# Half of x turned by transposing DMA, a shorter unfold and a new order of the queues, in a fused FFT filter and state-space kernel

## The chip, the cores and the metric

The kernel runs on one core of a Trainium2 chip. The metric is the device time of one execution in microseconds (us), the median of several runs. In the profile, PE is TensorE, PEld its weight loads, DVE is VectorE, ACT is ScalarE, POOL is GpSimd and SP is SyncE, whose queue issues nearly all DMAs here.

## The reference, cut to what matters

```python
# x: (1, 2048, 1024), bf16; S = 2048 rows, D = 1024 columns
g = sigmoid((x * gate_w).sum(-1))               # one gate for each row
a = irfft2(rfft2(x) * (w_r + 1j * w_i))         # a filter over both axes
Lam_bar = exp(dt * Lam)                         # P = 1024 complex states
Bu = einsum("bld,pd->blp", x, B_bar)
h[t] = Lam_bar * h[t - 1] + Bu[t]               # along the 2048 rows
b = 2 * einsum("blp,dp->bld", h, C).real + x * Dskip
return g * a + (1 - g) * b
```

## The kernel before

All of it is one program in which two branches share the engines. Rows of x come in sixteen row tiles of 128 rows (`r`), four to a chunk of 512 rows (`c`). States come in eight blocks of 128 (`jb`).

**Start.** SP loads the row tiles into `xn` (L445) and the first block of B into `bn`. `turn` (L478) transposes a tile: eight 128x128 transposes on PE into PSUM (`pt`, L483), and one copy of the result into `xT[c]`, by DVE (L488) or ACT (L486) in turn. `halves(c)` (L499) folds the columns of `xT[c]` into `xpm` on DVE, with one small product on PE (`xps`, L516) and its cast on ACT (L518).

**State-space branch.** `bu` (L862) multiplies `xT[c]` by a block of B, `BTs`, into PSUM (`psu`, L872; sixteen 512-column matmuls for a block and a chunk). ACT casts the result into `h` (L875). DVE rotates it by a table `cs` (`rot`, L840 to L846), scans along the rows (L884) and rotates it back by a table `pn` (`rot_out`). `load_BT` (L856) loads the later blocks of B by transposing DMA (L859), and `load_CT` those of C (L826). `table` (L614) makes `cs` and `pn[:, jb]` for each block.

**Filter branch.** Stage one: `fd` transforms along the columns (`ps_fd`, L651 and L656, from all of `xpm`), ACT casts (L662), `s1` does the first half of the row transform (L671), ACT casts (L674), and SP writes the result to the DRAM scratch `turn1` (L675). Stage two: `s2w` reads it back turned (L756, into slots that lie in `h`), does the second half (`ps_s`, L762), ACT casts to X2 (L765), and DVE multiplies by W (L767); `fixup` mends the first column through `Bcol` (L714). `is1` and `is2` are the inverse transforms (L780, L799), with another trip through DRAM between them, and `idft` (L814) ends the branch: ACT scales by the gate (L819) and SP writes `ga_scratch`.

**Output.** `unfold` (L907) reads two row tiles of `ga_scratch` and rebuilds the full 1024 columns from even and odd parts with two operations of 1024 elements (L915) and four of 512 (L919), two of which write backwards. `yout` (L926) multiplies `h` by C (`ps_y`, L935), adds the Dskip term (`diag`, L943, or L953 and L954) and combines both branches (L962 with an accumulating DMA from POOL, or L971 on DVE).

**What sets the order.** Nothing runs as written. Every operation is put into a `Plan` with an engine, a key and an estimated time; `Plan.run` (L237) simulates the engines by these estimates, takes the operation with the smallest key among those that could start, and emits each engine's queue in that order. The keys are linear in the constants `K_...` (L387 to L433). Buffers come from groups of slots handed out in that simulated order: two large buffers `b32` (`xn`, `xpm`, then the two halves of `h`), four PSUM slots, and so on. `ORDER` hands them out in the order in which they were made:

```python
ORDER = ("b32", "b8", "tf", "tt", "bt", "cs")
```

On the chip each engine then runs its queue in order and waits on semaphores.

Of the kernel before, what the change touches and what calls it, by code (L numbers as in the profile page):

```python
# [14 lines left out]
BF16 = mybir.dt.bfloat16  # L15
# [283 lines left out]
def kernel(  # L299
# [17 lines left out]
    nc = tc.nc  # L317
    x = A_x[0]
# [11 lines left out]
    cpool = ctx.enter_context(tc.tile_pool(name="cpool", bufs=1))  # L330
# [39 lines left out]
    def pe(key, us, fn, r=(), w=()):  # L370
        plan.op("PE", key, us + 0.16, fn, r, w, gap=us)
# [4 lines left out]
    def dve(key, us, fn, r=(), w=()):  # L376
        plan.op("DVE", key, us, fn, r, w, gap=us - 0.085)
# [4 lines left out]
    def dma(key, us, fn, r=(), w=(), eng="SP", issue=0.38):  # L382
        plan.op(eng, key, 0.0, fn, r, w, gap=issue, dma=us)

    U = 0.216
    A2 = nc.scalar.activation
    K_T0 = 103.63  # L387
    K_TB = 92.88
    K_D = 2317.44
    K_O = -4292.69  # L390
    K_TAB0 = -89.94
    K_TAB = -755.34
    K_F0 = 261.54
    K_F = 15.56
    K_W0 = -3804.78
    K_W = 211.26
    K_WI = -1048.11
    K_I0 = -7430.02
    K_I = 31.36
    K_ID = 61.05  # L400
    K_CT = 287.45
    K_FIX = -6993.11
    K_R1 = 218.2
    K_R2 = 3273.35
    K_RS = -1.13
    K_Y = -2754.69
    K_YS = 362.25
    K_H = 358.12
    K_HM = 136.71
    K_XR = -109.14  # L410
    K_HP = 257.29
    K_XP = -155.54
    K_XS = -637.95
    K_TP = -327.41
    K_DM = 2752.64
    K_BT = -203.64
    K_UN = 4095.78
    K_WD = -299.06
    K_KA = -1.48
    K_KR = -90.54  # L420
    K_YL = 2318.0
    K_PC = 2539.19
    K_TL = 361.21
    K_TM = 642.41
    K_D1 = 138.38
    K_WC = 442.52
    K_FW = -3775.02
    K_SM = -4700.75
    K_R3 = 2855.54
    K_R4 = -1680.01  # L430
    K_D3 = 231.26
    K_SK = -768.95
    K_GATE = 1276.71  # L433
    KX = lambda c: K_XP * (c > 0) + K_XS * max(c - 1, 0)


    vec8 = tile_of([8, 5, P], BF16, "vec8", "tt")
    for i, src in enumerate((B_Lambda_re, B_Lambda_im, B_log_dt, gate_w, B_Dskip)):
        dma(0, 0.05, lambda i=i, src=src: nc.scalar.dma_start(out=vec8.t[:, i, :], in_=src.rearrange("(j p) -> j p", p=P)),
            w=[(vec8, i)], eng="ACT", issue=0.33)  # L440

    xn = tile_of([P, 16, D], BF16, "xn", "b32")
    bn = tile_of([P, 2, D], BF16, "bn", "b8")
    for r in range(16):
        dma(r, 0.8, lambda r=r: nc.sync.dma_start(out=xn.t[:, r, :], in_=x[P * r:P * (r + 1), :]), w=[(xn, r)])  # L445
# [17 lines left out]
    ident = cpool.tile([P, P], BF16, name="ident")  # L463
# [11 lines left out]
    xT = [xpool.tile([P, 8, TC], BF16, name=f"xT{c}") for c in range(NCH)]  # L475
    BTb = {0: tile_of([P, 2, 8, P], BF16, "BTs", "bt")}

    def turn(key, src, item, dst, ditem, on_act):  # L478
        pt = psum([P, 8, P], "pt", BF16)

        def f():
            for j8 in range(8):
                nc.tensor.transpose(out=pt.t[:, j8, :], in_=src()[:, P * j8:P * (j8 + 1)], identity=ident)  # L483
        pe(key, 8 * 0.06, f, r=[item, ("ident",)], w=[(pt,)])
        if on_act:
            act(key, 1.01, lambda: nc.scalar.copy(out=dst(), in_=pt.t), r=[(pt,)], w=[ditem])  # L486
        else:
            dve(key, 0.69, lambda: nc.vector.tensor_copy(out=dst(), in_=pt.t), r=[(pt,)], w=[ditem])  # L488

    def turn_x(c):  # L490
        for q in range(4):
            r = 4 * c + q
            turn(KX(c) + q, lambda r=r: xn.t[:, r, :], (xn, r), lambda c=c, q=q: xT[c][:, :, P * q:P * (q + 1)],
                 ("xT", c, q), q % 2)

    xT_of = lambda c: [("xT", c, q) for q in range(4)]
    xpm = tile_of([P, 2, 4, S], BF16, "xpm", "b32")

    def halves(c):  # L499
        lo, hi = xT[c][:, 0:4, :], xT[c][:, 4:8, :]  # L500
        both = tile_of([P, 4, TC], BF16, "both", "su")
        at = slice(TC * c, TC * (c + 1))
        dve(KX(c) + K_H, 1.22, lambda: nc.vector.tensor_add(out=both.t, in0=lo, in1=hi), r=xT_of(c), w=[(both,)])
        for g, fn in enumerate((nc.vector.tensor_add, nc.vector.tensor_sub)):
            dve(KX(c) + K_H, 0.69, lambda g=g, fn=fn: fn(out=xpm.t[:, 0, 2 * g:2 * g + 2, at], in0=both.t[:, 0:2, :], in1=both.t[:, 2:4, :]),
                r=[(both,)], w=[(xpm, c, 0, g)])
# [101 lines left out]
            r=[("gB",)], w=[("omg_bf",)])  # L608
        dve(key + 30, 0.2, lambda: nc.vector.tensor_copy(out=omg, in_=omg_bf), r=[("omg_bf",)], w=[("omg",)])


    pn = cpool.tile([P, NJB, 2, TC], BF16, name="pn")

    def table(jb, key):  # L614
        tt = tile_of([P, 2, TC], FP32, "tt", "tt")
# [291 lines left out]
    def unfold(tb, key):  # L907
        eo = tile_of([P, 2, 2, K], BF16, "eoc", "eoc")
        dma(key - K_DM, 1.5, lambda: nc.sync.dma_start(out=eo.t.rearrange("p s h k -> p s (h k)"),
                                                       in_=ga_dram[P * tb:P * (tb + 2), :].rearrange("(s p) n -> p s n", s=2)),  # L910
            r=[("ga", bp) for bp in range(16)], w=[(eo,)], issue=0.55)
        pq = tile_of([P, 2, 2, K], BF16, "pq", "pq")
        ga = tile_of([P, 2, D], BF16, "ga", "bt")
        for i, fn in enumerate((nc.vector.tensor_add, nc.vector.tensor_sub)):
            dve(key, 0.69, lambda i=i, fn=fn: fn(out=pq.t[:, i], in0=eo.t[:, :, 0, :], in1=eo.t[:, :, 1, :]), r=[(eo,)], w=[(pq, i)])  # L915
        for i in range(2):
            for j, fn in enumerate((nc.vector.tensor_add, nc.vector.tensor_sub)):
                cols = slice(K * j, K * j + 256) if i == 0 else slice(K * j + 511, K * j + 255, -1)
                dve(key, 0.42, lambda i=i, cols=cols, fn=fn: fn(out=ga.t[:, :, cols], in0=pq.t[:, i, :, 0:256], in1=pq.t[:, i, :, 256:512]),  # L919
                    r=[(pq, i)], w=[(ga, i, j)])  # L920
        return ga

    dsk = tile_of([P, D], BF16, "dsk", "xs")
# [52 lines left out]

    KB = lambda p, cc: K_T0 + K_TB * (p + 0.5 * cc) + K_TL * (p >= 12) + K_TM * (p >= 14)
    KD = lambda p, c0: KB(p, 0) + K_D + K_KR * p + K_D1 * (c0 > 0)
    KF = lambda j: K_F0 + K_F * j
    KW = lambda b: K_W0 + K_W * b  # L980
    KI = lambda bp: K_I0 + K_I * bp
    halves(0)
    turn(5, lambda: bn.t[:, 0, :], (bn, 0), lambda: BTb[0].t[:, 0], (BTb[0], 0), 0)
    turn(5, lambda: bn.t[:, 1, :], (bn, 1), lambda: BTb[0].t[:, 1], (BTb[0], 1), 1)
    for c in range(1, NCH):
        turn_x(c)
        halves(c)
# [4 lines left out]
    def turns_of(lo, hi):  # L992
        for jb, c0, n, p in turns[lo:hi]:
            if c0 == 0:
                tabs[jb] = table(jb, K_TAB0 if jb == 0 else KB(p, 0) - K_TAB)
                if jb:
                    load_BT(jb, KB(max(p - 2, 0), 0) + K_BT)
            kd = KD(p, c0) + K_D3 * (c0 == 3)
            carries[jb] = bu(jb, c0, n, tabs[jb], carries.get(jb), (KB(p, 0), KB(p, 1)), kd)
            if c0 == 0:  # L1000
                if jb < 6:
                    rot_out(jb, 0, 2, KD(p, 0) + K_O)
                else:
# [71 lines left out]
```

## Time and profile before

| what | value |
|---|---|
| median of 3 runs | 321.35 us (321.22 to 322.42) |
| span of the profiled execution | 319.7 us |
| PE busy | 304.0 us, 95% |
| DVE busy | 296.0 us, 93% |
| ACT busy | 199.5 us, 62% |
| DMA, mean | 181 GB/s |

The span runs from the first to the last instruction of one profiled execution; the page gives no other time for that execution, and the runs' median is 1.65 us above the span. "Busy" is the union of an engine's instructions; matmuls are pipelined, and a matmul of 512 columns is shown as some 0.38 us long although the next one starts before it ends. In a row of groups, what follows the bar is busy time, mean ns of one, idle time of the engine just before, and who ended that idle time.

### The profile page before, as it was taken

To read this page: it belongs to the slowest core of one execution; us is meant where nothing else is said; L and a number is where in the kernel's file an instruction comes from. 1 tells how busy PE (TensorE), PEld (TensorE's weight loads), DVE (VectorE), ACT (ScalarE), POOL (GpSimd) and SP (SyncE) were. 2 spreads that over 40 slices of the span, in tenths; PEclk is the share of its full clock that TensorE was granted. 3 is DMA by queue.
4 is the path that set the end of the run, shared out by engine and by line. 5 is a ranking of instruction groups with operands and counts; after the bars stand their busy time and mean duration, and the time that the engine had idled before them with its cause. 6 is when DMAs were issued, how large, how long until landed. Compare 5 with 4: busy or idle time off the path is not lost.

```text
span 319.7 us, 5030 instructions
## 1 busy us (share of the span) xinstructions
PE 304.0 (95%) x1805; PEld 163.8 (51%) x1837; DVE 296.0 (93%) x439; ACT 199.5 (62%) x265; POOL 18.7 (6%) x28
## 2 busy tenths in 40 slices
PE   4889998999999999999999999999999999999994
PEld 4654575664444444444466756545544444444442
DVE  3999999998999999999999999999999999999433
ACT  3799999989999899799899998401132221100000
POOL 1000000000000000000000000000332331300000
PEclk9999999999999999999999999999999999999999
DMA  7996625998869999998599999991578774732002
GB/s 228 380 248 7 98 75 164 208 267 211 201 192 296 221 259 255 244 257 185 130 218 250 304 232 256 230 339 55 102 156 143 158 130 103 99 105 94 0 33 98
DMA packets 79984, 57.80 MB, mean 181 GB/s; under 512 B 49748, under 2 KB 65112, under 8 KB 79960
## 3 DMA queue, kind: packets, MB, share of 16 engines
q1 hardware_dynamic: 77000, 54.86, 68.3%
q0 software_dynamic: 2880, 2.62, 7.6%
q8 instruction: 14, 0.23, 0.3%
q14 instruction: 10, 0.08, 0.1%
q10 hardware_dynamic: 80, 0.01, 0.0%
HBM read 30.21 MB, written 16.78 MB: 147 GB/s over the span
## 4 chain that ended last, share of the span: by engine, by line
PE 58%; ACT 19%; DMA 13%; DVE 4%; issue 3%; SPq 2%; ACTq 0%
PE ps_y L935 34%; PE psu L872 14%; DMA xn<-in_A_x_dram 4%; DMA turn_scratch<-M_all 3%; ACT h L875 2%; ACT M_all L674 2%; PE ps_id L814 2%; DMA wA<-in_A_w_i_dram 2%; DMA h<-turn_scratch 2%; PE ps_s L762 2%; DMA Bcol<-turn_scratch 1%; PE ps_y L943 1%; ACT M_all L819 1%; ACT M_all L803 1%; ACT M_all L662 1%
## 5 line engine op out<-in xcount | busy, mean ns | idle before, releaser
L872 PE MATMUL psu<-xT,BTs 128*128 128x512 bf16 x497 | 115.9, 379 | 1.9 <-ACT G_all L674 0.5
L935 PE MATMUL ps_y<-CT,h 128*128 128x512 bf16 (+1 forms) x516 | 112.0, 372 | 2.0 <-DVE o L971 1.4
L935 PEld LDWEIGHTS <-h 128*128 128x128 bf16 x528 | 51.2, 98 | 57.6 <-issue 1.8
L872 PEld LDWEIGHTS <-BTs 128*128 128x128 bf16 x512 | 49.6, 98 | 58.7 <-issue 1.9
L884 DVE TENSOR_TENSOR_SCAN h<-r_sb,carry,h 128x512 bf16<-128x512 f32 x48 | 60.3, 1278 | 0.0
L962 ACT ACTIVATE y<-ps_y,omg 128x512 f32<-128x512 f32 x20 | 13.4, 687 | 57.7 <-PE ps_y L943 31.2
L875 ACT CAST h<-psu 128x1024 bf16<-128x1024 f32 x32 | 33.0, 1037 | 2.3 <-PE psu L872 2.2
L963 POOL DMA_DIRECT2D ga<-y x20 | 17.4, 891 | 257.7 <-DVE ga L919 227.2
L842 DVE TENSOR_TENSOR h<-h,su 128x1024 bf16<-128x1024 bf16 (+1 forms) x38 | 23.0, 606 | 0.1
L841 DVE TENSOR_TENSOR h<-h,pn 128x2048 bf16<-128x2048 bf16 (+1 forms) x20 | 20.2, 1009 | 0.0
L840 DVE TENSOR_TENSOR su<-h,pn 128x2048 bf16<-128x2048 bf16 (+1 forms) x20 | 20.2, 1008 | 0.0
L841 DVE TENSOR_TENSOR h<-h,cs 128x2048 bf16<-128x2048 bf16 (+1 forms) x18 | 19.9, 1104 | 0.1
L840 DVE TENSOR_TENSOR su<-h,cs 128x2048 bf16<-128x2048 bf16 (+1 forms) x18 | 19.7, 1096 | 0.0
L884 DVE TENSOR_TENSOR_SCAN h<-r_sb,h 128x512 bf16<-128x512 f32 x16 | 19.3, 1217 | 0.0
L784 ACT CAST h<-ps_is 128x1024 bf16<-128x1024 f32 x16 | 15.7, 1020 | 2.9 <-DVE wB L767 1.9
L765 ACT CAST h<-ps_s 128x1024 bf16<-128x1024 f32 x16 | 16.1, 1033 | 0.0
L819 ACT ACTIVATE M_all<-ps_id,gA 128x1024 bf16<-128x1024 f32 x13 | 15.4, 1181 | 0.6 <-PE ps_id L814 0.6
L483 PE MATMUL pt<-ident,xn 128*128 128x128 bf16 x128 | 9.9, 240 | 5.9 <-DMA xn<-in_A_x_dram 4.5
L971 DVE SCALAR_TENSOR_TENSOR o<-ps_y,omg,M_all 128x1024 bf16<-128x1024 f32 (+2 forms) x5 | 4.3, 861 | 11.6 <-PE ps_y L935 11.6
L674 ACT CAST M_all<-ps_s 128x1024 bf16<-128x1024 f32 x12 | 13.1, 1091 | 0.0
L483 PEld LDWEIGHTS <-xn 128*128 128x128 bf16 x128 | 8.8, 109 | 7.2 <-DMA xn<-in_A_x_dram 4.9
L662 ACT CAST M_all<-ps_fd 128x1024 bf16<-128x1024 f32 x11 | 11.6, 1066 | 1.2 <-DMA turn_scratch<-M_all 1.2
(138 smaller groups left out, 408.7 us busy)
## 6 DMA issues: line engine op xcount, KB each, us to landing
xn<-in_A_x_dram SPq DMA_DIRECT2D x16, 256.0 KB, 5.4
h<-turn_scratch SPq DMA_DIRECT2D x16, 256.0 KB, 5.5
turn_scratch<-h SPq DMA_DIRECT2D x16, 256.0 KB, 4.0
ga_scratch<-M_all SPq DMA_DIRECT2D x13, 256.0 KB, 3.5
turn_scratch<-M_all SPq DMA_DIRECT2D x12, 256.0 KB, 4.8
M_all<-turn_scratch SPq DMA_DIRECT2D x12, 256.0 KB, 3.0
M_all<-ga_scratch SPq DMA_DIRECT2D x6, 512.0 KB, 6.2
ga<-y POOLq DMA_DIRECT2D x20, 128.0 KB, 3.5
```

What stands on the lines that cost most here:

```text
L483: nc.tensor.transpose(out=pt.t[:, j8, :], in_=src()[:, P * j8:P * (j8 + 1)], identity=ident)
L674: act(key, 1.02, lambda: nc.scalar.copy(out=A1.t, in_=psa.t), r=[(psa,)], w=[(A1,)])
L765: act(key, 1.01, lambda: nc.scalar.copy(out=X2.t, in_=ps2.t), r=[(ps2,)], w=[(X2,)])
L819: act(key, 1.11, lambda: A2(out=eo.t, in_=pz.t, func=ACT.Copy, scale=gA[:, bp:bp + 1]), r=[(pz, 0), (pz, 1), ("gA",)], w=[(eo,)])
L840: dve(key, w, lambda: nc.vector.tensor_mul(out=sv(), in0=src()[:, ::-1], in1=bc(1)), r=sitem + [titem(1)], w=[(su,)])
L841: dve(key, w, lambda: nc.vector.tensor_mul(out=dst(), in0=src(), in1=bc(0)), r=sitem + [titem(0)], w=ditem)
L842: dve(key, h, lambda: nc.vector.tensor_add(out=dst()[:, 0], in0=dst()[:, 0], in1=sv()[:, 0]), r=[(su,)] + r0, w=r0)
L872: mm(psu.t[:, ri, :], lhsT=BT.t[:, ri, db, :], rhs=xT[c][:, db, :], start=(db == 0), stop=(db == 7))
L875: act(kb[cc] + K_KA, 1.01, lambda cc=cc, psu=psu: nc.scalar.copy(out=g()[:, :, cc, :], in_=psu.t), r=[(psu, 0), (psu, 1)], w=ui(cc) + ([(" ...
L884: dve(kd, 1.25, lambda cc=cc, ri=ri, carry=carry: nc.vector.tensor_tensor_scan(out=g()[:, ri, cc, :], data0=rb, data1=g()[:, ri, cc, :], i ...
L935: mm(psy.t[:, lo:hi], lhsT=hbuf[jb // 4].t[:, jb % 4, ri, P * tb:P * (tb + 1)], rhs=CT[pc].t[:, ri, jb % 2, lo:hi], start=(jb == 0 and ri ...
L963: dma(key - 1, 1.3, lambda cols=cols, y32=y32: nc.gpsimd.dma_start(out=ga.t[:, tb % 2, cols], in_=y32.t, accum_op=ALU.add), r=[(y32,)] + [ ...
```

## The change

Row tiles 8 to 15 (chunks 2 and 3) are no longer loaded as they are and turned on PE: SP issues a transposing DMA from x straight into `xT[c]`. The eight tiles that are still turned on PE land in `pn`, the slots of the tables, which are written later, instead of in a `b32` buffer of their own. `unfold` does its work in four operations of 1024 elements: the reversal moves into the write of `pq`, and both quarters of a half are then written in one operation. All 47 constants of the keys have new values, and two are new (`K_XD`, `K_XQ`, for the transposing loads), so the order of all queues is another one.

```diff
-    K_T0 = 103.63
-    K_TB = 92.88
-    K_D = 2317.44
...
+    K_T0 = 17.12
+    K_TB = 125.24
+    K_D = 14850.58
...
+    K_XD = 8.56
+    K_XQ = -0.0
...
-    xn = tile_of([P, 16, D], BF16, "xn", "b32")
+    pn = cpool.tile([P, NJB, 2, TC], BF16, name="pn")
+    xn = lambda r: pn[:, r % NJB].rearrange("p i t -> p (i t)")
...
-    for r in range(16):
-        dma(r, 0.8, lambda r=r: nc.sync.dma_start(out=xn.t[:, r, :], in_=x[P * r:P * (r + 1), :]), w=[(xn, r)])
+    xn_item = lambda r: [("pn", r % NJB, i) for i in range(2)]
+
+    def load_x(r):
+        dma(r, 0.8, lambda: nc.sync.dma_start(out=xn(r), in_=x[P * r:P * (r + 1), :]), w=xn_item(r))
+
+    for r in range(NJB):
+        load_x(r)
...
     def turn_x(c):
         for q in range(4):
             r = 4 * c + q
-            turn(KX(c) + q, lambda r=r: xn.t[:, r, :], (xn, r), lambda c=c, q=q: xT[c][:, :, P * q:P * (q + 1)],
+            if c >= 2:
+                dma(K_XD + K_XQ * r, 1.45, lambda r=r, q=q: nc.sync.dma_start_transpose(
+                    out=xT[c][:, :, P * q:P * (q + 1)], in_=x[P * r:P * (r + 1), :]), w=[("xT", c, q)], issue=1.36)
+                continue
+            turn(KX(c) + q, lambda r=r: xn(r), xn_item(r), lambda c=c, q=q: xT[c][:, :, P * q:P * (q + 1)],
                  ("xT", c, q), q % 2)
...
+        quarters = lambda v: v.rearrange("p s (h n) -> p s h n", h=2)
         for i, fn in enumerate((nc.vector.tensor_add, nc.vector.tensor_sub)):
-            dve(key, 0.69, lambda i=i, fn=fn: fn(out=pq.t[:, i], in0=eo.t[:, :, 0, :], in1=eo.t[:, :, 1, :]), r=[(eo,)], w=[(pq, i)])
-        for i in range(2):
-            for j, fn in enumerate((nc.vector.tensor_add, nc.vector.tensor_sub)):
-                cols = slice(K * j, K * j + 256) if i == 0 else slice(K * j + 511, K * j + 255, -1)
-                dve(key, 0.42, lambda i=i, cols=cols, fn=fn: fn(out=ga.t[:, :, cols], in0=pq.t[:, i, :, 0:256], in1=pq.t[:, i, :, 256:512]),
-                    r=[(pq, i)], w=[(ga, i, j)])
+            dve(key, 0.69, lambda i=i, fn=fn: fn(out=quarters(pq.t[:, i])[:, :, :, ::1 - 2 * i], in0=quarters(eo.t[:, :, 0, :]),
+                                                 in1=quarters(eo.t[:, :, 1, :])), r=[(eo,)], w=[(pq, i)])
+        for j, fn in enumerate((nc.vector.tensor_add, nc.vector.tensor_sub)):
+            dve(key, 0.69, lambda j=j, fn=fn: fn(out=quarters(ga.t[:, :, K * j:K * (j + 1)]), in0=pq.t[:, :, :, 0:256].rearrange("p i s n -> p s i n"),
+                                                 in1=pq.t[:, :, :, 256:512].rearrange("p i s n -> p s i n")),
+                r=[(pq, 0), (pq, 1)], w=[(ga, 0, j), (ga, 1, j)])
```

The new order of the start, as it stands in the changed program: SP issues four tiles of x, the two parts of `bn`, four tiles of x, then three transposing loads of x, the `BTs` pair of block 1, five transposing loads of x, and after these `G_all`, `TF_sb`, `TK_sb`, `Wc`, `dsk` and the `BTs` pair of block 2. Up to its first `ps_fd`, PE has 80 transposes of tiles (144 before) and 96 matmuls of `psu` (88 before).

More of the change, by code (lines that the diff above doesn't have):

```diff
@@ L386 @@
     A2 = nc.scalar.activation
-    K_T0 = 103.63
-    K_TB = 92.88
-    K_D = 2317.44
[L390 to L433, printed above, removed]
+    K_T0 = 17.12
+    K_TB = 125.24
+    K_D = 14850.58
+    K_O = -1473.38
+    K_TAB0 = -1033.78
+    K_TAB = -4884.09
+    K_F0 = 205.58
+    K_F = 18.95
+    K_W0 = -20711228042315.83
+    K_W = 8000.46
+    K_WI = 3390.37
+    K_I0 = -61551.62
+    K_I = 2265.53
+    K_ID = 2857.71
+    K_CT = 3100.75
+    K_FIX = -4086.22
+    K_R1 = -1544.1
+    K_R2 = 53784.63
+    K_RS = 1659.42
+    K_Y = -771.69
+    K_YS = 199.23
+    K_H = 14971.43
+    K_HM = 10328.26
+    K_XR = -2516.79
+    K_HP = -126.43
+    K_XP = -10079.29
+    K_XS = -2277.11
+    K_TP = -25309.1
+    K_DM = 3449318.56
+    K_BT = -2618.67
+    K_UN = 21537022.07
+    K_WD = -490.95
+    K_KA = -155075.5
+    K_KR = 2096.08
+    K_YL = 3600.97
+    K_PC = 547.04
+    K_TL = 3409.48
+    K_TM = 11845.92
+    K_D1 = 9114.34
+    K_WC = 3042.34
+    K_FW = 471.29
+    K_SM = -1948.3
+    K_R3 = -4108.58
+    K_R4 = 2987.05
+    K_D3 = 27477.4
+    K_SK = 132.19
+    K_XD = 8.56
+    K_XQ = -0.0
+    K_GATE = 963.36
     KX = lambda c: K_XP * (c > 0) + K_XS * max(c - 1, 0)
@@ L483, in f @@
                 nc.tensor.transpose(out=pt.t[:, j8, :], in_=src()[:, P * j8:P * (j8 + 1)], identity=ident)
-        pe(key, 8 * 0.06, f, r=[item, ("ident",)], w=[(pt,)])
+        pe(key, 8 * 0.06, f, r=item + [("ident",)], w=[(pt,)])
         if on_act:
@@ L609, in gates @@
         dve(key + 30, 0.2, lambda: nc.vector.tensor_copy(out=omg, in_=omg_bf), r=[("omg_bf",)], w=[("omg",)])
-    pn = cpool.tile([P, NJB, 2, TC], BF16, name="pn")
     def table(jb, key):
@@ L982 @@
     halves(0)
-    turn(5, lambda: bn.t[:, 0, :], (bn, 0), lambda: BTb[0].t[:, 0], (BTb[0], 0), 0)
-    turn(5, lambda: bn.t[:, 1, :], (bn, 1), lambda: BTb[0].t[:, 1], (BTb[0], 1), 1)
+    turn(5, lambda: bn.t[:, 0, :], [(bn, 0)], lambda: BTb[0].t[:, 0], (BTb[0], 0), 0)
+    turn(5, lambda: bn.t[:, 1, :], [(bn, 1)], lambda: BTb[0].t[:, 1], (BTb[0], 1), 1)
     for c in range(1, NCH):
```

## The prediction

> **What bounds the kernel now.** I read the page's busy times first, then the table by stretches, then the timeline around the start and around the hand-over between the two big stages.
>
> ```profile
> span 319.7 us, 5030 instructions
> ...
> PE 304.0 (95%) x1805; PEld 163.8 (51%) x1837; DVE 296.0 (93%) x439; ACT 199.5 (62%) x265; POOL 18.7 (6%) x28
> ```
> ```profile
> 0.00:10.00 10.00, 5.03 (x54) 4.30 (x55) 4.52 (x14) 3.89 (x5) 1.35 (x8) 1.00 0.77 252
> 10.00:20.00 10.00, 8.73 (x103) 6.56 (x105) 9.26 (x29) 8.45 (x14) 0.00 (x0) 1.00 1.13 327
> 40.00:60.00 20.00, 18.99 (x120) 12.89 (x122) 19.97 (x26) 19.96 (x24) 0.00 (x0) 1.00 0.48 138
> 100.00:120.00 20.00, 19.89 (x92) 8.93 (x93) 19.38 (x24) 18.22 (x27) 0.00 (x0) 1.00 1.09 263
> 200.00:220.00 20.00, 19.89 (x105) 10.04 (x107) 19.98 (x35) 3.68 (x4) 0.00 (x0) 1.00 0.84 245
> 280.00:300.00 20.00, 19.89 (x96) 9.43 (x97) 19.08 (x30) 0.00 (x0) 0.00 (x0) 1.00 0.24 80
> ```
> The columns after each stretch are its length and the busy us of PE, PEld, DVE, ACT and POOL, then clock, DMA share and GB/s. From 100 us on PE is full (19.89 of 20). Its losses lie in the first 20 us (6.2 us idle) and in 40 to 60 us, where ACT is the full engine (19.96) and PE is not. DVE is nearly full until 300 us. So the time is PE's work, plus what PE loses in the start, plus what it loses where ACT or a transfer holds it. The span is 319.7 us and the median of the runs 321.35 us; I take the 1.65 us between them as fixed.
>
> **The start: what goes.** These rows are the timeline's.
>
> ```profile
> 10.40 1.89 PE L872 MATMUL psu<-xT,BTs 128*128 128x512 bf16 x7
> 12.13 1.50 PE L483 MATMUL pt<-ident,xn 128*128 128x128 bf16 x24
> 18.28 1.50 PE L483 MATMUL pt<-ident,xn 128*128 128x128 bf16 x24 [1.00 <-ACT xT L486]
> 37.88 1.22 DVE L840 TENSOR_TENSOR su<-h,cs 128x2048 bf16<-128x2048 bf16 x1
> 37.98 0.60 PE L651 MATMUL ps_fd<-G_all,xpm 128*128 128x256 bf16 x4
> ...
> 39.27 1.93 ACT L662 CAST M_all<-ps_fd 128x1024 bf16<-128x1024 f32 x2
> ```
> ```profile
> 107.67 5.18 PE psu L872 x24
> ```
> ```profile
> L488 DVE COPY xT<-pt 128x1024 bf16<-128x1024 bf16 x8 | 5.5, 688 | 4.7 <-PE pt L483 4.6
> L486 ACT COPY xT<-pt 128x1024 bf16<-128x1024 bf16 x8 | 7.8, 1012 | 3.3 <-PE pt L483 3.3
> ```
> Eight row tiles no longer pass PE. That is 64 transposes; 24 take 1.50 us with some 0.16 us of latency, 0.056 each, so 3.6 us of PE. It is also four copies on DVE (4 x 0.69 = 2.8 us) and four on ACT (4 x 1.01 = 4.0 us). A full 512-column matmul costs 5.18/24 = 0.216 us.
>
> The forward transform (`ps_fd`) needs all of `xpm`, thus all of x. In the new order PE has, from its first `psu` at 10.4 us (the loads ahead of that are the same ten in the same order), 24 transposes, 96 matmuls of `psu` (88 before) and 8 of `xps`: 1.35 + 104 x 0.216 = 23.8, so `ps_fd` at 34.2 us. DVE has four copies and one table operation (0.7) fewer ahead of its first rotation: 37.88 minus 3.1 (instructions overlap by some 0.07) is 34.8, and `xpm` is ready one operation earlier, 34.1. PE and DVE agree on 34.3 us, against 37.98 now. That holds only if the transposing loads are in time.
>
> **The start: what comes.** Eight transposing DMAs of 256 KB go on SP's queue, and two for `BTs` among them. They also stand ahead of `G_all`, `TF_sb`, `TK_sb`, the eight gathers of `Wc`, `dsk`, the next `BTs` pair and the first write of `turn1`.
>
> ```profile
> 13.31 1.48 SPq L859 DMA_TRANSPOSE BTs<-in_B_B_re_dram  x1
> ...
> 14.84 3.82 SPq L859 DMA_TRANSPOSE BTs<-in_B_B_im_dram  x1
> ...
> 19.87 5.35 SPq L694 DMA_DIRECT2D Wc<-in_A_w_r_dram  x4
> ...
> 25.27 5.01 SPq L694 DMA_DIRECT2D Wc<-in_A_w_i_dram  x4
> ...
> 32.60 1.25 SPq L859 DMA_TRANSPOSE BTs<-in_B_B_re_dram  x1
> ...
> 33.90 1.30 SPq L859 DMA_TRANSPOSE BTs<-in_B_B_im_dram  x1
> ```
> ```profile
> 16.00:17.00 1.00, 1.00 (x19) 0.91 (x17) 1.00 (x3) 0.99 (x2) 0.00 (x0) 1.00 0.98 359
> ...
> 34.00:35.00 1.00, 1.00 (x7) 0.43 (x5) 1.00 (x2) 1.00 (x3) 0.00 (x0) 1.00 1.07 177
> 35.00:36.00 1.00, 1.00 (x6) 0.45 (x5) 1.00 (x2) 1.00 (x3) 0.00 (x0) 1.00 1.05 227
> 36.00:37.00 1.00, 1.00 (x6) 0.49 (x5) 1.00 (x3) 0.97 (x3) 0.00 (x0) 1.00 1.14 176
> ```
> A `BTs` half has the same shape (128 rows of 1024). Its price from below is 1.30 us, the issue that nothing held up. From bytes: 34 to 37 us moved 0.58 MB at a full DMA share, 193 GB/s, so 1.36 us each. From above it is 2.65 us, the mean of the issues at 13.31 and 14.84; but there plain loads still filled the queue (359 GB/s at 16 us), so I take 1.36, the row it is nearest to. Ten plain loads (2.6 MB at 359 GB/s) end near 10.2 us; ten transposing ones at 1.36 end at 23.8, some 25 with the landing. DVE needs the last of x at 34.1 minus eight half-size operations, two table operations and one full one (7.5 us with overlaps): 26.6 us. So they are hidden, by 1.6 us, and begin to cost beyond 1.55 us each. SP is then free of them at 23 us; the gathers (10.4 us), the next pair (2.6) and four plain issues end near 38, when the first `turn1` write becomes ready.
>
> The Trainium skill, "Advanced Engine Details and Errata", section "X-Bar Transpose (TRN2)", says that such transfers are as fast as regular ones, 350 to 400 GB/s. This trace shows about half: 193 beside 359. By the page they would land some 6 us sooner and my sum would stay, as DVE and PE set 34.3; the rival of slow transposes would lose its chance. I keep to the rows.
>
> **The stage between.** From the first cast of `ps_fd` ACT is the full engine until the last write of `turn1`.
>
> ```profile
> 67.96 1.01 ACT L662 CAST M_all<-ps_fd 128x1024 bf16<-128x1024 f32 x1 [1.19 <-DMA turn_scratch<-M_all]
> ...
> 75.15 8.79 PE L872 MATMUL psu<-xT,BTs 128*128 128x512 bf16 x40
> ...
> 76.20 1.08 ACT L674 CAST M_all<-ps_s 128x1024 bf16<-128x1024 f32 x1
> ...
> 77.30 0.36 SPq L675 DMA_DIRECT2D turn_scratch<-M_all  x1
> ...
> 79.57 0.53 SPq L714 DMA_DIRECT2D Bcol<-turn_scratch  x1
> 80.19 2.37 SPq L756 DMA_DIRECT2D h<-turn_scratch  x3
> ...
> 86.33 1.46 PE L762 MATMUL ps_s<-h,TK_sb 128*128 128x512 bf16 x6
> ...
> 88.38 2.35 DVE L767 TENSOR_TENSOR wA<-h,wA 128x2048 bf16<-128x2048 bf16 x2
> ```
> ```profile
> DMA to landing us min/median/max: 3.6/5.5/6.2
> ```
> The last row is the landing of `h<-turn_scratch`, L756. ACT took 39.27 to 77.28, 38.0 us. The new order has two casts of `psu` fewer there and 1.0 us of table work more: 37.0 us. It begins at 34.3 + 1.1 = 35.4 and ends at 72.4. PE has only 80 `psu` matmuls between the first `ps_fd` and the first `ps_s` of the second stage (112 before), so it waits more for ACT in this stage: part of the gain is given back here. After the last cast, the write lands 2.3 us later (77.28 to 79.57), the read is issued 0.6 later and takes 3.6: 78.9. PE's own queue says the same: its last `ps_s` of this stage ends 2.1 us before ACT's, at 70.3, and 40 matmuls of `psu` follow: 78.9.
>
> From `ps_s` at 86.33 to the end were 233.4 us. The new order leaves 24 more `psu` matmuls and a small fix-up for that part, 5.4 us: 78.9 + 233.4 + 5.4 = 317.7 us. That is 2.0 us less than 319.7, so 321.35 - 2.0 = 319.3 us.
>
> **Unfold, slots, keys.**
>
> ```profile
> L915 DVE TENSOR_TENSOR M_all<-M_all 128x1024 bf16<-128x1024 bf16 x6 | 4.2, 705 | 0.0
> ...
> L919 DVE TENSOR_TENSOR ga<-M_all 128x512 bf16<-128x512 bf16 x16 | 6.7, 442 | 0.0
> ...
> L884 DVE TENSOR_TENSOR_SCAN h<-r_sb,carry,h 128x512 bf16<-128x512 f32 x48 | 60.3, 1278 | 0.0
> ```
> ```profile
> 308.47 1.28 DVE L971 SCALAR_TENSOR_TENSOR o<-ps_y,omg,M_all 128x1024 bf16<-128x1024 f32 x1 [9.36 <-PE ps_y L935]
> ```
> Unfold goes from 2 x 0.70 + 4 x 0.44 to 4 x 0.70, so 0.36 us less, eight times 2.9 us. Half of the 0.44 us operations already write backwards at the same price, so I price the reversed write at 0.70. I count nothing for it: DVE stands idle for 9.36 us before its last group, and PE is the full engine there. If the reversed write cost double, 8 x 0.7 = 5.6 us would still fit. x landing in `pn` frees a large buffer for `h` from the start; the first `psu` cast can move ahead of x, and that is in the order counted above. Keys only choose the order; the one loss that I see is DVE's. From its first rotation to the first product with W it took 50.5 us (37.88 to 88.38). Four scans (5.1 us), a rotation (1.22 + 2 x 0.69) and two table operations (1.4) that stood there now stand behind, so it arrives at 34.8 + 41.4 = 76.2 us. But X2 is there only 2.05 us after `ps_s` starts (86.33 to 88.38), at 81: DVE idles 5 us, and 9 us of its work comes after.
>
> **Rivals.** First, *late transposes*, slower: at 2.0 us each they land at 10.2 + 20 + 1 = 31.2, 4.6 late, and `ps_fd`, ACT's stage and all behind move with it: 323.9 us. At 2.2 us each it is 325.9. It decides from 1.55 us on. For it: the 3.82 us issue; against it: 1.30 and 193 GB/s.
>
> Second, *the gain is lost in the stage between*, no change. ACT waits for slots whose writes stand behind twenty W loads on SP, as at 67.96 (1.19 us); two such waits more, or DVE coming late to row tile 8 after its 5 us idle, cost 2 to 3 us: 321.3 to 322.3. For it: ACT's queue is denser than before, and PE now waits there for it.
>
> Third, a page's rule. By rows a transpose of eight blocks costs 1.30 us of issue; were it one block at a time at that price, 64 blocks would take 83 us, and `ps_fd` would start near 100 us, some 386 us in all. The Trainium skill, "VectorE: DVE Perf Modes", sections "The three transpose paths" and "Rules for kernel authors", has a block at 1309 ns by DMA and advises TensorE where PSUM will do. The trace speaks against blocks in a row: the pair issued from 32.6 on had moved by 37 us.
>
> **Chances.** My forecast 0.55, late transposes 0.22, lost in between 0.22, the page's rule 0.01. A run counts as changed beyond 0.5% (1.6 us), about what a measurement can tell. The forecast lies only 0.4 us beyond that, so 0.09 of its 0.55 falls within; 0.17 of the second and 0.03 of the late ones too. So faster 0.46, within 0.29, slower 0.25. The range begins at 315.5: were PE held in the stage no more than now, it would need the 48.4 us between 37.98 and 86.33 less 32 matmuls and the fix-up (7.1), and `ps_s` would start at 75.6, which gives 316.0. It ends at 325.5, transposes at 2.2 us.
>
> **What would show it.** Right: no transposes for chunks 2 and 3; `ps_fd` at 34 to 35 us; last x landed before 27; `ps_s` of the second stage near 79; PE full from 100 us; DVE idle some 5 us before the first product with W. Wrong: `ps_fd` held by a DMA of `xT`, an issue of those transposes over 1.6 us each, or PE waiting for `h` from DVE after 200 us.

## The result, and the profile after

| kernel | median, us | runs | ratio to before | 95% interval |
|---|---|---|---|---|
| before | 321.52 | 4 (321.22 to 322.42) | 1 | |
| changed | 318.06 | 4 (317.07 to 319.10) | 0.9891 | 0.9858 to 0.9923 |
| changed, timed again | 317.82 | 6 (317.33 to 318.88) | 0.9885 | 0.9866 to 0.9905 |

The changed kernel is 1.1% faster, 3.5 us by the medians. The forecast was 319.3 us, a gain of 2.0. The profiled execution took 319.1 us with a span of 317.1 us, 2.6 less than before; the forecast had the span at 317.7.

The page's first rows, busy time and share of each engine, and the chain that ended last:

```profile
span 317.1 us, 4908 instructions
...
PE 302.6 (95%) x1773; PEld 160.5 (51%) x1773; DVE 293.6 (93%) x419; ACT 196.3 (62%) x261; POOL 18.7 (6%) x28
...
PE 73%; ACT 12%; DMA 10%; issue 2%; DVE 1%; SPq 1%; ACTq 0%
```

PE holds 73% of the chain; DVE, nearly as busy, 1%. The table by stretches, with the columns of the prediction:

```profile
10.00:20.00 10.00, 10.00 (x71) 5.47 (x70) 8.57 (x23) 7.74 (x13) 0.00 (x0) 1.00 1.18 192
...
40.00:60.00 20.00, 16.82 (x107) 11.40 (x106) 19.78 (x25) 20.00 (x25) 0.00 (x0) 1.00 0.95 244
...
100.00:120.00 20.00, 18.65 (x108) 7.95 (x107) 20.00 (x25) 18.98 (x27) 0.00 (x0) 1.00 1.08 249
```

From 10 to 20 us PE is full, 10.00 against 8.73. From 40 to 60 us it is idle longer than before, 3.2 us against 1.0, while ACT has no gap at all. From 100 to 120 us it loses 1.35 us, against 0.1. The gain of the start is given back in part in these two stretches.

The timeline at the start, and from the end of stage one on:

```profile
10.33 1.89 PE L883 MATMUL psu<-xT,BTs 128*128 128x512 bf16 x8
...
12.05 1.50 PE L491 MATMUL pt<-ident,pn 128*128 128x128 bf16 x24
...
21.14 0.68 DVE L522 TENSOR_TENSOR xpm<-xT 128x1024 bf16<-128x1024 bf16 x1
...
23.32 5.34 PE L883 MATMUL psu<-xT,BTs 128*128 128x512 bf16 x24
...
26.93 1.28 DVE L522 TENSOR_TENSOR xpm<-xT 128x1024 bf16<-128x1024 bf16 x2
...
34.11 0.60 PE L667 MATMUL ps_fd<-G_all,xpm 128*128 128x256 bf16 x4
...
34.88 1.21 DVE L851 TENSOR_TENSOR su<-h,cs 128x2048 bf16<-128x2048 bf16 x1
35.22 1.02 ACT L673 CAST M_all<-ps_fd 128x1024 bf16<-128x1024 f32 x1
```
```profile
64.77 1.23 DVE L851 TENSOR_TENSOR su<-h,cs 128x2048 bf16<-128x2048 bf16 x1 [3.31 <-ACT cs L640]
...
69.20 8.80 PE L883 MATMUL psu<-xT,BTs 128*128 128x512 bf16 x40
...
69.89 1.11 ACT L685 CAST M_all<-ps_s 128x1024 bf16<-128x1024 f32 x1
...
77.83 1.03 PE L773 MATMUL ps_s<-h,TK_sb 128*128 128x512 bf16 x4
```

`ps_fd` starts at 34.11 us (37.98 before), and stage two's `ps_s` at 77.83 (86.33 before), with 32 `psu` matmuls fewer between the two. From there to the end of the span are 239.3 us.

SP's queue:

```profile
6.27 6.83 SPq L502 DMA_TRANSPOSE xT<-in_A_x_dram  x3
...
16.50 6.71 SPq L502 DMA_TRANSPOSE xT<-in_A_x_dram  x5
...
24.90 7.69 SPq L705 DMA_DIRECT2D Wc<-in_A_w_r_dram  x4
32.63 5.82 SPq L705 DMA_DIRECT2D Wc<-in_A_w_i_dram  x4
...
42.62 0.53 SPq L686 DMA_DIRECT2D turn_scratch<-G_all  x1
```

Five transposing loads in a row take 6.71 us, 1.34 each; the first three, behind the plain loads, 2.28 each. The ten are issued by 23.2 us.

### The profile page after: what moved, and what is told of

Its sections match the earlier page's. It is cut to its first block, busy times and chain, and to the rows that moved or that the text cites. A ratio compares the mean times of both kernels' runs of the same rounds, so it can differ in the third digit from the quotient of the medians.

```text
span 317.1 us, 4908 instructions
## 1 busy us (share of the span) xinstructions
PE 302.6 (95%) x1773; PEld 160.5 (51%) x1773; DVE 293.6 (93%) x419; ACT 196.3 (62%) x261; POOL 18.7 (6%) x28
## 4 chain that ended last, share of the span: by engine, by line
PE 73%; ACT 12%; DMA 10%; issue 2%; DVE 1%; SPq 1%; ACTq 0%
PE ps_y L947 35%; PE psu L883 25%; PE ps_id L825 4%; ACT M_all L685 3%; ACT M_all L673 3%; DMA pn<-in_A_x_dram 3%; PE ps_is L810 2%; DMA Bcol<-turn_scratch 2%; PE ps_is L791 2%; PE ps_is L792 2%; DMA wB<-in_A_w_i_dram 2%; DMA wA<-in_A_w_r_dram 1%; PE ps_y L955 1%; DMA wA<-in_A_w_i_dram 1%; DVE o L983 1%
## 5 line engine op out<-in xcount | busy, mean ns | idle before, releaser
L685 ACT CAST M_all<-ps_s 128x1024 bf16<-128x1024 f32 x13 | 14.7, 1130 | 0.0
L830 ACT ACTIVATE M_all<-ps_id,gA 128x1024 bf16<-128x1024 f32 x12 | 13.8, 1153 | 0.0
L983 DVE SCALAR_TENSOR_TENSOR o<-ps_y,omg,M_all 128x1024 bf16<-128x1024 f32 (+2 forms) x6 | 5.6, 928 | 8.2 <-PE ps_y L947 7.6
L673 ACT CAST M_all<-ps_fd 128x1024 bf16<-128x1024 f32 x11 | 12.3, 1127 | 0.0
L662 PE MATMUL ps_fd<-G_all,xpm 128*128 128x256 bf16 x64 | 9.4, 272 | 2.7 <-ACT M_all L685 2.1
L855 DVE TENSOR_TENSOR h<-su,h 128x1024 bf16<-128x1024 bf16 (+1 forms) x20 | 11.5, 574 | 0.0
```

The costliest lines, as they stand in the source:

```text
L673: act(key, 1.02, lambda: nc.scalar.copy(out=X1.t.rearrange("p c (n g r) -> p c n g r", g=2, r=2), in_=pf.t.rearrange("p r g c n -> p c n g ...
L685: act(key, 1.02, lambda: nc.scalar.copy(out=A1.t, in_=psa.t), r=[(psa,)], w=[(A1,)])
```

## The experiments

Most of the variants below keep the planner's order: its estimates are left as they were, and only what an operation emits is changed. So the queues stand as in the changed kernel, but for the instructions named. The two kernels with exchanged keys are reordered throughout. Unless another view is named, the rows below are from the timeline of the kernel just told of: start, length, engine, line, operation, and in brackets the idle time before it with what ended it.

**The changed kernel again.**

> The changed kernel itself, timed again beside the variants. Both theories: 318.1 us, span 317.1, first ps_fd at 34.1 us, first ps_s of the second stage at 77.8.

317.82 us, 0.9885. In this profiled execution `ps_fd` started a microsecond earlier, and next to nothing of it was left at `ps_s`, as its timeline shows:

```profile
33.09 0.60 PE L667 MATMUL ps_fd<-G_all,xpm 128*128 128x256 bf16 x4
...
61.75 1.01 ACT L673 CAST G_all<-ps_fd 128x1024 bf16<-128x1024 f32 x1 [0.83 <-DMA turn_scratch<-G_all]
...
77.71 1.03 PE L773 MATMUL ps_s<-h,TK_sb 128*128 128x512 bf16 x4
```

ACT waited 0.83 us for a slot whose `turn1` write stood behind the W loads; `ps_s` came 0.1 us earlier, not 1.0. This is the wait of the prediction's second rival.

**Is the removed work what brings the gain?** The work is put back as repeats, and the loads, the landing slots and the order stay.

```diff
+        again = 2 if len(item) == 2 else 1
-            for j8 in range(8):
+            for j8 in again * list(range(8)):
...
-            act(key, 1.01, lambda: nc.scalar.copy(out=dst(), in_=pt.t), ...
+            act(key, 1.01, lambda: [nc.scalar.copy(out=dst(), in_=pt.t) for _ in range(again)], ...
```

> The changed kernel with the removed work put back as repeats: the eight tiles that still pass PE are transposed twice and copied twice (64 more transposes on PE, four more copies on DVE, four on ACT), transposing loads and all orders kept. Theory (the 3.6 us of transposes are what ps_fd came forward by, and ACT and all behind it follow): ps_fd 3.6 us later, near 37.7, ps_s near 81.4, span near 320.7. Rival (the new order of the queues carries the gain, PE had room at the start): ps_fd less than 1.5 us later and the span below 318.6.

323.59 us, 1.0054 (1.0033 to 1.0074); 1.7% above the changed kernel and slower than before. Its timeline:

```profile
11.11 1.89 PE L884 MATMUL psu<-xT,BTs 128*128 128x512 bf16 x7
...
12.83 2.84 PE L492 MATMUL pt<-ident,pn 128*128 128x128 bf16 x48
...
36.55 0.60 PE L668 MATMUL ps_fd<-G_all,xpm 128*128 128x256 bf16 x4
...
81.08 1.03 PE L774 MATMUL ps_s<-h,TK_sb 128*128 128x512 bf16 x4
```

`ps_fd` is 2.4 us later than 34.11 (I expected 3.6), `ps_s` 3.3 later, the span 4.8 (321.9). The repeats do not stand where the removed work stood: 40 of the 64 come ahead of the first `psu`, where PE waits for x, and delay it by only 0.8 us (11.11 beside 10.33); the other 24 take 1.34 us (2.84 beside 1.50). Behind `ps_s`, up to 120 us, PE waits 1.2 us more than in the changed kernel, above all for reads of the scratch (2.8 beside 1.6 by the table of waits). So the theory holds in kind: with the work back, the gain is gone. It also shows that the new order with the transposing loads does not help without the removal: it has 2.2 us more span than before (321.9 beside 319.7).

The two halves, each alone: the loop repeated but not the copies, and the copies but not the loop.

> Half of put_back: the eight tiles that still pass PE are transposed twice (64 more transposes on PE, 3.6 us), but copied once. put_back moved ps_fd by 2.5 us (34.1 to 36.55), ps_s by 3.3 and the span to 321.9. Theory (PE and DVE agree at the start, as forecast, so either alone sets ps_fd): ps_fd at 35.5 to 36.5 us, span near 320. Rival (the copies carry it, PE still has room between its waits): ps_fd below 34.6, span within 1 us of 317.

322.97 us, 1.0031 (1.0006 to 1.0056). Its timeline:

```profile
36.59 0.60 PE L668 MATMUL ps_fd<-G_all,xpm 128*128 128x256 bf16 x4
```

> The other half of put_back: the eight tiles are transposed once but copied twice (four more copies on DVE, 2.8 us, and four on ACT, 4.0 us). Theory (PE and DVE agree at the start): ps_fd at 35.5 to 36.5 us, span near 320. Rival (PE's 3.6 us carry it): ps_fd below 34.6, span within 1 us of 317.

320.80 us, 0.9965 (0.9946 to 0.9985); span 319.0. Its table by stretches from 10 to 20 us:

```profile
10.00:20.00 10.00, 8.73 (x57) 4.81 (x56) 8.05 (x19) 6.40 (x10) 0.00 (x0) 0.84 1.17 177
```

PE's half alone moves `ps_fd` as far as both do. The copies moved it too, to 36.88, but in that execution the granted clock was 0.84 from 10 to 20 us, so this is no clean reading. Its times are: the other eleven executions had a clock of 0.999 or 1, and the median is 0.8% above the changed kernel, against 1.5% for PE's half. The halves' 1.5% and 0.8% add to more than the 1.7% of both, so they overlap: each alone delays the kernel, PE's more. That fits "PE and DVE agree", but the second half also holds four copies on ACT, and DVE's share of it was not tried by itself.

**How late may the transposing loads be?**

```diff
+    def x_by_dma(r, out):
+        for q in range(4 - 4, 4) if r == 8 else ():
+            nc.sync.dma_start_transpose(out=xT[3][:, :, P * q:P * (q + 1)], in_=x[0:P, :])
+        nc.sync.dma_start_transpose(out=out, in_=x[P * r:P * (r + 1), :])
...
```

> The changed kernel with four more transposing loads of 256 KB ahead of the eight on SP's queue (rows 0 to 127 of x, into the places that the last four of the eight overwrite), order kept. Each costs 1.34 us of issue, so the last of x is issued 5.4 us later, at 28.6 us. Theory (slack of 1.6 us, then one for one): ps_fd 3.8 us later, at 37.9 us, ps_s at 81.6 and the span near 320.9. Rival 1 (no slack): 5.4 us later, 322.5. Rival 2 (the loads are hidden far more deeply, PE has other work): ps_fd stays, 317.1.

324.64 us, 1.0095 (1.0072 to 1.0119); span 322.4. Its timeline:

```profile
22.13 6.73 SPq L501 DMA_TRANSPOSE xT<-in_A_x_dram  x5
...
23.61 1.90 PE L887 MATMUL psu<-xT,BTs 128*128 128x512 bf16 x8 [2.96 <-DMA BTs<-in_B_B_re_dram]
...
26.07 0.69 DVE L526 TENSOR_TENSOR xpm<-xT 128x1024 bf16<-128x1024 bf16 x1 [3.79 <-DMA xT<-in_A_x_dram]
...
32.23 1.29 DVE L526 TENSOR_TENSOR xpm<-xT 128x1024 bf16<-128x1024 bf16 x2 [0.29 <-DMA xT<-in_A_x_dram]
32.25 1.67 PE L887 MATMUL psu<-xT,BTs 128*128 128x512 bf16 x7 [0.37 <-DMA xT<-in_A_x_dram]
...
39.58 0.60 PE L671 MATMUL ps_fd<-G_all,xpm 128*128 128x256 bf16 x4
```

The chain that ended last has this piece:

```profile
27.56 4.55 DMA xT<-in_A_x_dram
```

`ps_fd` is 5.5 us later: the first rival (no slack, 5.4), not the 3.8 of the theory. The rows say why. The four loads delay everything behind them on SP's queue, and PE and DVE wait three times: PE for the `BTs` pair (2.96 us), both for the last tile of chunk 2 (26.07), and both again for the last tile of all. That last one was issued at 27.56 and was there at 32.11, 4.55 us later; from 32.25 to `ps_fd` PE works without a gap. So the last tile sets `ps_fd` here.

In the changed kernel the last tile is issued at 21.87. PE is the first to need it, for the last eight of the 24 matmuls that start at 23.32: sixteen of them at 0.216 us come before, so they begin at 26.8. DVE follows at 26.93. With the 4.55 us of this run the tile would be there at 26.4; gathers_on_pool, below, shows another 4.0 us after its issue, which would make 25.9. That leaves 0.4 to 0.9 us of slack. The last tile of chunk 2 was used 3.9 us after its issue here (22.13 to 26.07). Issued at 16.50 it would be there at some 20.4, and DVE uses it at 21.14: 0.7 us. These are estimates from three landings; which of the two tiles has less room in the changed kernel is not shown.

**Unfold.** Old form, same order:

```diff
-            ... out=quarters(pq.t[:, i])[:, :, :, ::1 - 2 * i] ...
+            ... out=quarters(pq.t[:, i]) ...
-            dve(key, 0.69, lambda j=j, fn=fn: fn(out=quarters(ga.t[:, :, K * j:K * (j + 1)]), ...
+            cols = lambda i, j: slice(K * j, K * j + 256) if i == 0 else slice(K * j + 511, K * j + 255, -1)
+            dve(key, 0.69, lambda j=j, fn=fn: [fn(out=ga.t[:, :, cols(i, j)], ...) for i in range(2)], ...
```

> The changed kernel with the old six-operation unfold put back, in place, with the order of every queue kept: 8 x 0.36 = 2.9 us more on DVE, after 170 us or so. Theory (unfold counted at nothing, PE is the full engine there): span 317.1 within 0.5, ps_fd and ps_s unmoved, and DVE's idle time before its last group falls from 4.95 us to about 2. Rival (DVE, busy 93 %, sets the second half): 2.9 us later, span near 320.

318.84 us, 0.9909 (0.9881 to 0.9938), which overlaps the changed kernel's 0.9866 to 0.9905; span 317.1, the same. The costliest groups, second half of unfold (busy us and mean ns behind the bar), in the changed kernel and then in this one:

```profile
L930 DVE TENSOR_TENSOR ga<-G_all 128x1024 bf16<-128x1024 bf16 x10 | 6.8, 683 | 0.0
...
L930 DVE TENSOR_TENSOR ga<-M_all 128x1024 bf16<-128x1024 bf16 x6 | 4.1, 680 | 0.0
```
```profile
L931 DVE TENSOR_TENSOR ga<-G_all 128x512 bf16<-128x512 bf16 x20 | 7.4, 416 | 0.0
...
L931 DVE TENSOR_TENSOR ga<-M_all 128x512 bf16<-128x512 bf16 x12 | 4.5, 413 | 0.0
```

In this order the old form costs 11.9 us of DVE against 10.9, some 1.0 us more and not 2.9, and the end does not move.

**The stage between.** Four casts more on ACT:

```diff
-        act(key, 1.02, lambda: nc.scalar.copy(out=A1.t, in_=psa.t), ...
+        act(key, 1.02, lambda: [nc.scalar.copy(out=A1.t, in_=psa.t) for _ in range(2 if 4 <= j < 8 else 1)], ...
```

> The changed kernel with four of the sixteen casts after s1 (row tiles 4 to 7) done twice, orders kept: four more operations on ACT, at the 0.905 us that lie between two starts there, 3.6 us. Theory (from the first cast of ps_fd to the last write of turn1 ACT is the full engine and all behind follows it): the last s1 cast ends 3.6 us later, near 74.6, ps_s starts near 81.4 and the span is near 320.7. Rival (PE's own queue sets ps_s): ps_s less than 1.5 us later, span below 318.6.

322.45 us, 1.0018 (0.9988 to 1.0047), 1.3% above the changed kernel. Its timeline:

```profile
73.84 1.06 ACT L685 CAST M_all<-ps_s 128x1024 bf16<-128x1024 f32 x1
...
81.91 1.03 PE L773 MATMUL ps_s<-h,TK_sb 128*128 128x512 bf16 x4
```

The last cast and `ps_s` are 4.0 and 4.1 us later, and the span is 3.0 longer (320.1). In this execution ACT's stage began 0.7 us earlier (34.52), so it was 4.6 us longer for four casts priced at 3.6; a repeated pair takes 1.97 us from start to start, which makes a repeat 1.06 and the four 4.3. What ACT gets more in this stage goes to `ps_s`; PE's queue hides none of it.

Then less work instead of more. Three table operations of block 1 go to POOL:

```diff
-        act(key, 1.04, lambda: nc.scalar.copy(out=cs.t, in_=tf.t), ...
+        act(key, 1.04, lambda: (nc.gpsimd.tensor_copy if jb == 1 else nc.scalar.copy)(out=cs.t, in_=tf.t), ...
...
+        act(key + K_TP, 0.72, lambda: (nc.gpsimd.tensor_scalar(out=kk(), in0=sn_f(), scalar1=at(ci), ...) if jb == 1 else
...
+        act(key + K_TP, 0.72, lambda: (nc.gpsimd.tensor_scalar(out=rr(), in0=cs_f(), scalar1=at(ci), ...) if jb == 1 else
...
```

> The changed kernel with three of ACT's table operations of row tile 1 (two scalings of 128x512 and the cast of cs, 0.62 + 0.62 + 0.91 us between starts, at 53 to 55 and 63.6 us) on POOL, all orders kept. Theory (ACT is the full engine from 35 to 71 us, and four casts more moved ps_s by 4.1): the last s1 cast ends up to 2.2 us earlier, near 69, ps_s near 76 and the span near 315; DVE's wait of 3.3 us for cs goes. Rival 1 (ACT then waits for turn_scratch writes that stand behind the W loads, as it did for 0.8 us where it started 1 us earlier): ps_s 0 to 1 us earlier, span above 316. Rival 2 (POOL's operations are slow, or slow DVE down): ps_s later than 77.8.

319.51 us, 0.9915 (0.9883 to 0.9946); span 317.8: no gain. Its timeline:

```profile
62.82 1.01 ACT L675 CAST G_all<-ps_fd 128x1024 bf16<-128x1024 f32 x1 [2.00 <-DMA turn_scratch<-G_all]
...
77.85 1.03 PE L775 MATMUL ps_s<-h,TK_sb 128*128 128x512 bf16 x4
```

The first rival: ACT, with 2.2 us less to do, waits 2.00 us for the same write behind the W loads, and `ps_s` stands where it stood. So this stage seems to have two limits at the same place, ACT's own work and the writes' place on SP's queue.

To take the second away too, the first `wB` loads went to POOL's queue:

```diff
+        que = nc.gpsimd if b == 2 else nc.sync
...
+                nc.gpsimd.tensor_copy(out=home(b).t[:, 0, 0:1], in_=xpm.t[:, 0, 3, S - 1:S])
...
```

> table_on_pool with, besides, the eight loads of the first wB moved from SP's queue, where they stand ahead of seven turn1 writes (3.75 us of issue), to POOL's, started when the last quarter of xpm is there. Theory (both ACT and the writes' place behind the W loads hold the stage): ACT waits for no write, ps_s near 75.5 to 76 and the span 314.5 to 315.5, where table_on_pool alone gets less. Rival (the writes have room, or PE is full before that): same as table_on_pool within 0.5 us.

320.98 us, 0.9959 (0.9934 to 0.9983): a miss. That it is slower than table_on_pool is not shown: eight of its twelve executions had a mean granted clock of 0.995, and the median of the four at 1 is 319.0 us, against 319.5 there, where all seven were at 1. One row of its timeline tells how it differs:

```profile
50.56 1.01 ACT L687 CAST G_all<-ps_s 128x1024 bf16<-128x1024 f32 x1 [2.42 <-DMA turn_scratch<-G_all]
```

The wait for a write did not go but came 12 us earlier. The `wB` loads are now issued from 38 us on, ahead of the first write, which is itself issued at 45.44 (42.62 in the changed kernel), behind a `BTs` load whose issue took 3.94 us (2.00); that the `wB` loads slow these down is what I take from it, not shown. In this execution `ps_fd` also started 1.8 us later, before POOL issued anything, so its span of 319.5 is no clean reading. It stays open whether both limits can be moved together; no variant beat the changed kernel.

**SP's queue at its worst place.** The gathers of `Wc` go to POOL's queue:

```diff
+                        if i + odd + e == 0:
+                            nc.gpsimd.tensor_copy(out=Wc[:, 0, 0:1], in_=xT[3][:, 0, TC - 1:TC])
+                            nc.gpsimd.memset(Wc, 0.0)
...
-                            nc.sync.dma_start(out=Wc[lo:lo + 32, e, odd:odd + 32], ...
+                            nc.gpsimd.dma_start(out=Wc[lo:lo + 32, e, odd:odd + 32], ...
```

> The changed kernel with the eight gathers of Wc moved from SP's queue (where their issue took 12.2 us, 23.9 to 36.1) to POOL's, started there once the last tile of x has landed; all other orders kept. The first write of turn1, at 42.0 us now, can go when its cast is done, near 39, and the W loads behind it 2 to 3 us earlier. Theory (SP's queue, 4 us later than forecast, is what holds ACT's slots and the first loads of W): ACT's wait of 0.8 us for turn_scratch and PE's and DVE's waits for wA and wB between 80 and 110 us shrink, span 316 or a little less, 0.5 to 1.5 us faster than the changed kernel. Rival 1 (all of that is hidden behind PE's 40 matmuls ahead of ps_s): within 0.5 us of 316.7 to 317.1. Rival 2 (the gathers now run beside other transfers and delay them): slower.

319.32 us, 0.9917 (0.9883 to 0.9950); span 316.8: the first rival, no gain. Its timeline, POOL's start and SP's queue:

```profile
25.78 0.52 POOL L705 COPY Wc<-xT 128x1 bf16<-128x1 bf16 x1 [23.86 <-DMA xT<-in_A_x_dram]
...
38.85 0.39 SPq L686 DMA_DIRECT2D turn_scratch<-G_all  x1
...
45.27 0.36 SPq L686 DMA_DIRECT2D turn_scratch<-G_all  x1
45.68 0.46 SPq L757 DMA_DIRECT2D wA<-in_A_w_r_dram  x1
```

The first write goes 3.8 us earlier, but the fifth waits for its cast, and the W loads behind it start at 45.68, as in the changed kernel (after its fifth write, at 45.8). The late queue was hidden behind ACT's casts. The first row shows when the last tile of x is there: POOL waits for it and starts at 25.78, 4.0 us after its issue at 21.8 in this run.

**Form and keys, crossed.**

```diff
-    K_T0 = 17.12
-    K_TB = 125.24
+    K_T0 = 103.63
+    K_TB = 92.88
...
```

> The changed kernel's instructions (transposing loads, four-operation unfold, x in the tables' slots) ordered with the keys of before; only the two keys of the transposing loads are new. Theory (the instructions bring the gain at the start, and the order decides what is left of it): ps_fd starts as early as in the changed kernel, 34 us or earlier, but more than the 3.6 us is lost behind it, and the span is above 319.7, slower than before. Rival (the keys only trim): span within 1 us of the changed kernel, 316 to 318.

330.21 us, 1.0260 (1.0205 to 1.0315).

> The kernel before (all of x turned on PE, six-operation unfold) ordered with the new keys. Theory (the new order fits the new instructions alone): slower than before, span above 320.5. Rival (the new order is better by itself and carries part of the gain): span below 319.2, faster than before.

328.15 us, 1.0192 (1.0146 to 1.0238).

Both are slower than before, as the theory had it. What each does to the start is read from ACT's first cast of `ps_fd`, which needs the whole product (in both kernels the first `ps_fd` matmuls are those of the half of `xpm` that is ready early, so their start says less). First the new form with the old keys, then the old form with the new keys:

```profile
35.93 1.91 ACT L673 CAST M_all<-ps_fd 128x1024 bf16<-128x1024 f32 x2
```
```profile
38.80 1.90 ACT L662 CAST M_all<-ps_fd 128x1024 bf16<-128x1024 f32 x2
```

Before, this cast started at 39.27 us, in the changed kernel at 35.22. So the form moves the start by 3.3 us without the keys, and the keys alone by 0.5. The loss with the new form and the old keys is behind, where PE waits above all for the `h` that DVE has not rotated back yet (the table of waits, PE, from 120 us on):

```profile
PE ps_y L947 <- DVE h L853: 5.5, 1, 5.5
PE ps_id L825 <- ACT M_all L814: 2.8, 5, 1.1
```

These waits come to 11.0 us in all, against 1.4 in the changed kernel. The granted clock has a part in it too: in the stretch from 220 to 240 us, in which the longest wait ends, it was 0.83, and the four executions had a mean of 0.985 to 0.99.

The new form costs 2.6% with the old keys, the new keys cost 1.9% with the old form, and together they gain 1.1%.

## Why the prediction was right

**The start: right.** `ps_fd` was forecast at 34.3 us and came at 34.11; the first cast at 35.4 and came at 35.22; DVE's first rotation at 34.8 and came at 34.88. put_back and its halves show that the gain is gone when this work, PE's above all, is back; and the crossing shows that the form, not the order, moves the start.

**The loads: right on the price, too generous on the slack.** Forecast 1.36 us each, measured 1.34. The window from 10 to 20 us, full of transposing loads, moves 192 GB/s at a DMA share of 1.18, as the 193 of the prediction's rows. The Trainium skill, "Advanced Engine Details and Errata", section "X-Bar Transpose (TRN2)", has 350 to 400 GB/s; the traces of both kernels show about half of it. The first three took 2.28 us each, which by the prediction's own sign (over 1.6) spoke against it; but the last plain load of x was landing until 9.82 us, and the ten together were issued by 23.2, where the forecast had 23.8.

The step that failed is the slack. I gave 1.6 us, from 25 for the last landing to 26.6 for DVE's need. The landing was put too early, 1.2 us after the end of the issue; by the landings of late_four and gathers_on_pool it comes at 25.9 to 26.4. And I asked only when DVE needs the tile, not PE, which comes to it a little earlier, at 26.8. That leaves 0.4 to 0.9 us, and the last of chunk 2 has 0.7. Over the ten loads that carry it, 0.4 to 0.9 us is 0.04 to 0.09 each: by this estimate the rival of late transposes decides from some 1.4 us on, not 1.55. With 1.34 measured it lost by little, and that the loads stayed hidden was in part luck.

**SP's queue: wrong by 4 us, without effect.** Free at 38 us by the forecast, at 42.6 in fact: the gathers took 13.5 us of issue and not 10.4, and `dsk` and the `BTs` pair some 4. gathers_on_pool shows no gain when the first write goes 3.8 us earlier.

**The stage between: right in kind, 1.2 us too long.** ACT took 35.8 us (35.22 to 71.0), not 37.0. I carried over the 38.0 us of before whole, and in them its wait of 1.19 us for `turn_scratch`; in the changed kernel ACT does not wait there. So `ps_s` came at 77.83 and not 78.9. That PE would wait more for ACT is seen: 3.2 us idle from 40 to 60 us.

**The rest: right in the sum, with some luck.** 238.8 us forecast from `ps_s` to the end, 239.3 measured. 77.83 + 239.3 = 317.1. But PE was not full from 100 us on, as forecast: it lost 1.35 us up to 120. From 120 to 300 us it then lost nothing, where it had lost 1.9 us before (178.10 of 180 us busy), so two differences offset each other in part. The span was 0.6 us shorter than forecast. The other 0.7 us is the step from span to median: I added 1.65 us as fixed, but that is the median of several runs less the span of one of them. In every run on record an execution's time lies 1.7 to 2.2 us above its own span. The changed kernel's median lies only 1.0 us above 317.1, as the profiled execution (319.1) was itself 1.0 us above the median. The forecast gain of 2.0 us was thus short of the 3.5 by the medians and the 2.6 by the spans. The range had a slip: by the prediction's own sum its upper end is 325.9 us, not 325.5.

**Unfold: right that it counts for nothing; its size depends on the order.** In the kernel before, its operations kept DVE busy for 24.5 us (11.2 at L915, 13.3 at L919), in the changed kernel for 21.8, so 2.7 us less where I had 2.9. But the old form in the new order, unfold_six, costs only 1.0 us more than the new: its halves last 0.415 us each, not 0.44, and take 0.37 of busy time each, as they overlap. Why they were longer before is not shown. The price of the reversed write was right: four operations of 0.68.

**DVE's idle time: wrong on the wait.** It was to idle 5 us before the first product with W, for X2, and this sign did not come. It idles 3.31 us up to 64.77, for the table `cs` from ACT, works on from there, and reaches the product at 80.08 (forecast 81).

**The rivals.** Late transposes did not happen. The wait of the second rival exists, but here it takes away only what would come in excess: it appears where ACT is 1 us early (0.83) or has 2.2 us less to do (2.00). The third rival fell: a tile of eight blocks has an issue of 1.34 us, not eight times that.

**What the prediction left out** is the crossing of form and keys. "Keys only choose the order" is true, but the form gains nothing without them, nor they without the form: 327.4 us of span with either alone, beside 319.7 before and 317.1 with both. The prediction was safe from this only because it read the new order instead of assuming the old one. The landing of x in the tables' slots was not tried by itself.

## What to carry to other kernels

Price a change in the order in which it will really run; moving work off the full engine paid here only once the queues had been fitted to it. For loads that feed a chain, work out the slack of each batch where any engine first needs it, from the landing and not from the end of the issue. Where a stage is timed from its total in the trace of before, take the waits out of that total first.

## What the hardware showed that I had not expected

Work moved to POOL slowed DVE down. In table_on_pool POOL ran from 53.59 to 57.7 us (timeline):

```profile
53.59 1.58 POOL L641 TENSOR_SCALAR tt<-tf,co 128x512 f32<-128x512 f32 x1 [51.65 <-DMA wA<-in_A_w_i_dram]
...
53.76 1.60 DVE L897 TENSOR_TENSOR_SCAN h<-r_sb,carry,h 128x512 bf16<-128x512 f32 x1
55.28 1.11 DVE L645 SCALAR_TENSOR_TENSOR pn<-tf,co,tt 128x512 bf16<-128x512 f32 x1
56.76 1.50 DVE L648 SCALAR_TENSOR_TENSOR pn<-tf,ncr,tt 128x512 bf16<-128x512 f32 x1 [0.37 <-POOL tt L643]
```

In the changed kernel the same three take 1.28, 0.75 and 0.75 us: 1.4 us less. The Trainium skill, "SBUF — State Buffer", section "Who interferes with whom", says that a DVE instruction with two SBUF inputs contends with a GpSimd instruction that reads SBUF; these rows agree. And each scaling took POOL 1.57 to 1.58 us where ACT had 0.62 between two starts.

The start of one and the same program varies by a microsecond: in the two profiled executions of the changed kernel `ps_fd` came at 34.11 and at 33.09 us, and `ps_s` all the same at 77.83 and 77.71. In the five variants that leave the start as it is, `ps_fd` came at 33.41 to 34.16 us four times, and in table_and_wB_on_pool at 35.93. So the shifts of `ps_fd` by 2.4 to 2.8 us in put_back and its halves, single executions each, carry the argument only together with the medians.
